# Forgetting attention and a gated convolution layer on one core: even partitions of q and k written by DMA, later weight loads, and the last output accumulated gate by gate

## The chip, the cores and the metric

The kernel runs on one core of a Trainium2 chip. The core has TensorE (PE), VectorE (DVE), ScalarE (ACT), GpSimd (POOL) and SyncE (SP), which here only issues DMAs, and 16 DMA engines. The metric is the device time in microseconds of one execution; a kernel's time is the median of its runs. A profile is of one execution and shows what each engine did when.

## The reference

Eight batches of eight heads, sequence length 576, head size 64. Attention with a forgetting gate comes first, and its heads side by side are the input of a feed-forward layer whose hidden units are gated by a convolution over the sequence.

```
scores = q @ k.T / 8
cum    = cumsum(log(clip(f, 1e-4, 1)))
scores = where(causal, -1e9, scores + cum[row] - cum[col])
x      = softmax(scores) @ v                  # heads side by side: (8, 576, 512)
h      = relu(x @ w_in)                       # 1024 hidden units
conv   = w[0]*h[s-1] + w[1]*h[s] + w[2]*h[s+1]
out    = (h * sigmoid(conv)) @ w_out          # (8, 576, 512), float32
```

## The kernel before

**Units of work.** A half batch `hb` is four heads of one batch; there are 16. Each has a q tile `stq` and a k tile `stk` of 128 partitions by 2304 columns (four heads of 576 positions) in bfloat16, in a ring of four buffers. All names and lines in this section are those of the kernel before.

**q and k in bfloat16 without a cast.** `load_qk` (L196) lets a DMA transpose read the float32 inputs as 16-bit halves. A head's 64 float32 values become 128 partitions: an odd partition holds the upper half of a value, which is the value in bfloat16, and an even one the lower half, which is no number. So the even partitions have to be overwritten before a matmul contracts over the 128 partitions. `clamp` (L202) does that in place, half a tile at a time (128 x 1152, so four calls for a half batch): it multiplies each partition by 1 or 0 and adds a constant, which leaves the odd partitions, clears the even ones and writes ones into two rows of `stq` (2 and 4) and minus one into row 0 of `stk`.

**The decay is in the same matmul.** With `kc`, the cumulated logarithm scaled for q's and k's side in two bfloat16 parts, copied to DRAM as `kd`, `rows_of` (L208, L210) writes one row of it to partition 0 of `stq` and two to partitions 2 and 4 of `stk`. The matmul over 128 partitions (L305) then gives the score with decay. Half batch 0 doesn't wait for that and adds the decay with two more matmuls each (L308, L310). The maximum isn't subtracted.

**Attention of a half batch.** Scores go to PSUM as a tail block, diagonal blocks and blocks off the diagonal. ScalarE takes the exponential (L317, L342, L332). GpSimd applies the causal mask to tail and diagonal blocks (L320, L345). For a whole batch, PE adds up the columns with a matrix of ones (`sums`), VectorE transposes and inverts the sums (L376, L377) and spreads them (L380); PE multiplies by v (`pv`), and VectorE normalises into `xt` (L389). v is loaded by `load_v` (L218) in five DMAs for a half batch, one for each block of 128 positions, and cast to float16 (L224, L226) on VectorE or GpSimd.

**Feed-forward of a batch.** For each of eight blocks `ff` of hidden units: PE multiplies by `w_in` (L399), ScalarE takes relu (L403), VectorE makes the convolution in two operations (L409, L411), ScalarE a tanh (L414), and VectorE forms the gated value `hg` (L418). When all eight are there, PE multiplies by `w_out` (L425, L430), ScalarE copies PSUM out (L438), and SP stores (L446, L449).

**The order of the work.** Nothing is scheduled at run time. `Plan` plays through all tasks of the kernel with assumed durations, keys as due times, and counts of free buffers, and so fixes each engine's order and, where a task may go to one of two engines, the engine. The instructions are then emitted in that order, and each engine works through its own in order. A DMA's issue holds its place in the queue of the engine that issues it: SP issues transposes, v and the output; POOL issues `kd`'s rows and the weights, which it converts to float16 on the way (L465); ACT issues a few at the start. A task waits for its inputs and for its buffers through semaphores. In `ps_t` there are four PSUM tiles of 1024 columns.

**Clamps' engine.** In half batches 1 and 2 a clamp may go to VectorE or GpSimd, and in all later ones it goes to GpSimd.

Of the kernel before, what the change touches and what calls it, by code (L numbers as in the profile page):

```python
# [11 lines left out]
BF16 = mybir.dt.bfloat16  # L12
# [102 lines left out]
def kernel(  # L115
# [21 lines left out]
    NFF = D_FF // 128  # L137
    SCALE = float(1.0 / (D ** 0.5))
    NHB = BH // 4
    HH = 4  # L140
    HS = HH * S
    RING, NP, NPT, NVA, NVF, NHT, NU, NOB = 4, 6, 4, 4, 3, 4, 3, 3
    AB = 256
# [7 lines left out]
    kd = dpool.tile([2, BH, S], BF16, name="kd")  # L151
# [8 lines left out]
    kc = cpool.tile([128, S], BF16, name="kc")  # L160
# [43 lines left out]

    def rows_of(hb):
        tq, tk = stq_t[hb % RING], stk_t[hb % RING]
        c = slice(hb * HH, (hb + 1) * HH)
        nc.gpsimd.dma_start(tq[0:1, 0:HS], kd[0:1, c, :].rearrange("j h s -> j (h s)"))  # L208
        row = HS + 64
        nc.gpsimd.dma_start(bass.AP(tensor=tk.tensor, offset=int(tk.offset) + 2 * row, ap=[[2 * row, 2], [1, HS]]),  # L210
                            kd[:, c, :].rearrange("j h s -> j (h s)"))

    def load_v(hb, t_load, eng):
        vf = vf_t[slot[t_load, "vf"]]
        base = int(v.offset) + hb * HH * S * D
        for kb in range(NKB):
            n = 128 if kb < NKB - 1 else SL
            eng.dma_start(vf[0:n, :, kb, :],  # L218
                          bass.AP(tensor=v.tensor, offset=base + kb * 128 * D, ap=[[D, n], [S * D, HH], [1, D]]))
# [17 lines left out]

    nc.gpsimd.iota(lii[:, 0:1], pattern=[[0, 1]], base=0, channel_multiplier=1)
# [23 lines left out]
    for t in range(RING):  # L262
        nc.gpsimd.memset(stk_t[t][:, HS:HS + 64], 0.0)
# [4 lines left out]
    nc.scalar.dma_start(kd[0], kc[0:BH])  # L268
    nc.scalar.dma_start(kd[1], kc[BH:128])
# [191 lines left out]
    def weights(pieces, dst, src, after, key, width):  # L461
        made = []
        for w in range(pieces):
            made.append(add({"POOL": 0.9}, after, key + 0.1 * w,
                            lambda me, w=w: nc.gpsimd.dma_start(  # L465
                                dst[:, :, width * w:width * (w + 1)],
                                src[:, :, width * w:width * (w + 1)]),
                            lag=2.0, dma=6.0 / pieces))
        return made
# [4 lines left out]
    for hb in range(NHB):  # L474
# [17 lines left out]
        if hb == 0:  # L492
            t_rows[hb] = None
        else:
            cl = []
            for p in range(2):
                for s in range(2):
                    cl.append(add({"POOL": 1.35, "DVE": 0.6} if hb < 3 else {"POOL": 1.35}, [t_ld[hb, s]], base - 1.0 + 0.1 * (2 * p + s),
                                  (lambda e, me, hb=hb, p=p, s=s: clamp(hb, p, s, e)) if hb < 3 else (lambda me, hb=hb, p=p, s=s: clamp(hb, p, s, nc.gpsimd))))
            t_rows[hb] = add({"POOL": 1.1}, cl, base - 0.8, lambda me, hb=hb: rows_of(hb), lag=2.5)  # L500
# [57 lines left out]
    for b in range(B):  # L558
        k1 = 4 * b + 5.0
        us = {}  # L560
        for ff in range(NFF):
# [12 lines left out]
            else:  # L574
# [3 lines left out]
                               give=[("ht", x)])  # L578
        done = [gates[b, ff] for ff in range(NFF)]
        for c in range(5):  # L580
            key = k1 + 4.2 + 0.8 * c
            if c in (0, 2, 4):
                t_o = x = add({"PE": 1.75 if c < 4 else 0.95}, done + t_wout, key,
                              lambda me, g0=g0, c=c: ffn2(me, g0, c), take=["ps"],
                              give=[("hg", g0)] if c == 4 else [])
            else:
                x = add({"PE": 1.75}, done, key, lambda me, t_o=t_o, g0=g0, c=c: ffn2(t_o, g0, c), behind=[t_o])
            if c in (1, 3, 4):
# [44 lines left out]
```

## Time and profile before

| | us |
|---|---|
| median of three runs | 336.97 |
| the runs | 333.33, 336.97, 337.31 |
| the profiled execution's own time | 335.01 |
| its span, first to last instruction | 333.3 |
| mean granted PE clock (1 is full) | 0.923 |

A page of the profile gives for each engine the time in which it was busy, its share of the span and the number of instructions. A group is all instructions of one line, engine and operation, with their tiles ("output<-inputs"), count, total and mean time. In a timeline a line gives the start, the time and the engine of one or more instructions that follow each other. A stage's line gives, for a stretch of the span, the busy time of PE, its weight loads (PEld), DVE, ACT and POOL with the number of instructions, and then the PE clock, the DMA engines' mean share and the rate in GB/s. The share of the DMA engines is the sum of their packets' times and can exceed 1 where packets overlap. A DMA queue's line gives its packets, its megabytes, and its packets' time as a share of 16 engines' span; q1 is SP's queue, q10 ACT's and q0 POOL's. A completion notice counts as a packet. Matmuls are pipelined, so a busy PE isn't one at its peak.

In this span the first L376 begins at 35.5 us and the others at 66.0, 104.9, 153.1, 191.6, 230.5, 262.6 and 291.7, one for each batch. The last gate (L418) ends at 320.8.

### The profile page before, as it was taken

Reading aid. Unit: us, or ns where it says so; the run is one execution under the profiler, and the core shown is the slowest. Engines: PE = TensorE matmul, PEld = TensorE weight load, DVE = VectorE, ACT = ScalarE, POOL = GpSimd, SP = SyncE. Lnnn points to the kernel's source line nnn. Section 1 sums busy time; section 2 is a strip of 40 time slices with the busy share of each in tenths; the row PEclk is TensorE's granted clock in tenths of the full one; section 3 lists DMA queues with packets and bytes.
Section 4 is the critical chain, followed back from the end, with each engine's and each line's share of the span. In section 5 each row is a group of like instructions: output and inputs, shape, how many; then the busy total and the mean of one; then the engine's idle time right before and its main releaser. Section 6 shows DMA issues by size and latency. Waiting matters only on the chain.

```text
span 333.3 us, 6984 instructions
## 1 busy us (share of the span) xinstructions
PE 259.6 (78%) x2832; PEld 177.3 (53%) x2832; DVE 279.2 (84%) x319; ACT 201.0 (60%) x267; POOL 184.8 (55%) x193
## 2 busy tenths in 40 slices
PE   0777956394955699699929998299979999979964
PEld 0555744273743564368704777147755775755622
DVE  4473899199999999897997799988999899799940
ACT  3166666373757674377906877178757888906822
POOL 4097799989999889304984069822881221100000
PEclk9997999698678989799996999879999999997979
DMA  8999999989996793319961589017301201100303
GB/s 174 232 195 194 196 198 195 197 133 221 220 177 104 94 218 96 120 65 223 149 140 63 83 177 181 2 65 151 73 4 63 76 9 63 66 18 0 128 16 142
DMA packets 126182, 40.97 MB, mean 123 GB/s; under 512 B 118693, under 2 KB 121893, under 8 KB 126150
## 3 DMA queue, kind: packets, MB, share of 16 engines
q1 hardware_dynamic: 118592, 37.76, 53.3%
q0 software_dynamic: 7232, 2.31, 6.2%
q10 hardware_dynamic: 326, 0.45, 0.5%
q8 instruction: 22, 0.36, 0.5%
q14 instruction: 10, 0.08, 0.1%
HBM read 14.15 MB, written 9.58 MB: 71 GB/s over the span
## 4 chain that ended last, share of the span: by engine, by line
DVE 38%; PE 35%; SPq 11%; issue 5%; DMA 4%; ACT 4%; POOL 2%; DVEq 0%; POOLq 0%; ACTq 0%
PE ps L425 13%; DVE hg L418 10%; DVE u L409 9%; PE ps L399 9%; SPq L196 8%; DVE u L411 8%; PE ps L366 7%; PE ps L305 5%; DVE va L224 3%; DMA vf<-in_v_dram 3%; DVE xt L389 3%; SPq L218 3%; DVE rb L380 2%; DVE va L226 1%; DMA stk<-kd 1%
## 5 line engine op out<-in xcount | busy, mean ns | idle before, releaser
L305 PE MATMUL ps<-stq,stk 128*128 128x128 bf16 (+3 forms) x576 | 64.7, 254 | 31.5 <-DVE stq L202 10.6
L399 PE MATMUL ps<-xt,w_in_f 128*128 128x288 f16 x512 | 77.5, 303 | 13.3 <-ACT ht L403 8.5
L414 ACT ACTIVATE hg<-u,cw 128x576 f16<-128x576 f32 x64 | 49.5, 776 | 62.2 <-DVE u L411 62.0
L425 PE MATMUL ps<-w_out_f,hg 128*128 128x512 f16 x256 | 66.7, 415 | 21.0 <-DVE hg L418 17.3
L418 DVE SCALAR_TENSOR_TENSOR hg<-hg,ht 128x576 f16<-128x576 f16 x64 | 67.1, 1057 | 9.1 <-ACT hg L414 8.9
L332 ACT ACTIVATE pp<-ps 128x1024 f16<-128x1024 f32 x64 | 64.1, 1022 | 12.2 <-PE ps L305 10.1
L409 DVE SCALAR_TENSOR_TENSOR u<-ht,cwt 128x576 f32<-128x576 f16 x64 | 67.5, 1066 | 4.4 <-ACT ht L403 4.4
L399 PEld LDWEIGHTS <-w_in_f 128*128 128x128 f16 x512 | 51.6, 103 | 33.6 <-issue 14.7
L411 DVE SCALAR_TENSOR_TENSOR u<-ht,cwt,u 128x576 f32<-128x576 f16 x64 | 65.7, 1037 | 0.8
L305 PEld LDWEIGHTS <-stk 128*128 128x128 bf16 x576 | 41.5, 104 | 44.3 <-issue 12.6
L345 POOL TENSOR_SCALAR_AFFINE_SELECT pp<-pd 128x1024 f16<-128x1024 f32 x32 | 39.6, 1236 | 33.8 <-ACT pd L342 33.1
L425 PEld LDWEIGHTS <-hg 128*128 128x128 f16 x256 | 26.3, 105 | 55.2 <-DVE hg L418 20.0
L202 POOL TENSOR_SCALAR stk<-stk,lim 128x1152 uint16<-128x1152 uint16 x29 | 50.5, 1744 | 0.5 <-DMA stk<-in_k_dram 0.5
L202 POOL TENSOR_SCALAR stq<-stq,lim 128x1152 uint16<-128x1152 uint16 x28 | 46.1, 1646 | 4.9 <-DMA stq<-in_q_dram 2.8
L403 ACT ACTIVATE ht<-ps 128x576 f16<-128x576 f32 x64 | 41.0, 651 | 12.4 <-PE ps L399 12.1
L320 POOL TENSOR_SCALAR_AFFINE_SELECT pt<-p 128x256 f16<-128x256 f32 x16 | 11.0, 689 | 60.1 <-ACT p L317 60.1
L342 ACT ACTIVATE pd<-ps 128x1024 f32<-128x1024 f32 x32 | 32.7, 1023 | 3.8 <-PE ps L305 2.1
L366 PE MATMUL ps<-pp,ones_h 128*64 128x128 f16 (+3 forms) x576 | 28.6, 249 | 1.0 <-POOL pp L345 0.6
L438 ACT COPY ob<-ps 128x1024 f32<-128x1024 f32 (+1 forms) x24 | 19.1, 796 | 14.7 <-PE ps L425 13.5
L366 PEld LDWEIGHTS <-ones_h 128*64 128x64 f16 x640 | 24.0, 116 | 7.0 <-issue 4.3
L366 PE MATMUL ps<-pp,va 128*64 128x128 f16 (+3 forms) x576 | 25.5, 241 | 2.6 <-DVE xt L389 2.6
L366 PEld LDWEIGHTS <-va 128*64 128x64 f16 x640 | 22.6, 111 | 6.7 <-issue 4.8
(66 smaller groups left out, 200.1 us busy)
## 6 DMA issues: line engine op xcount, KB each, us to landing
vf<-in_v_dram SPq DMA_DIRECT2D x64, 128.0 KB, 3.0
out_dram<-ob SPq DMA_DIRECT2D x16, 512.0 KB, 3.0
vf<-in_v_dram SPq DMA_DIRECT2D x16, 64.0 KB, 3.4
w_in_f<-in_moe_w_in_dram POOLq DMA_DIRECT2D x4, 256.0 KB, 5.6
w_out_f<-in_moe_w_out_dram POOLq DMA_DIRECT2D x4, 256.0 KB, 5.3
out_dram<-ob SPq DMA_DIRECT2D x16, 64.0 KB, 2.2
fsb<-in_f_dram ACTq DMA_DIRECT2D x2, 144.0 KB, 4.1
stq<-in_q_dram SPq DMA_TRANSPOSE x17, 5.9
```

Of the source, the lines that this page charges most:

```text
L202: eng.tensor_scalar(t, t, lim[:, 2 * side:2 * side + 1], lim[:, 2 * side + 1:2 * side + 2], op0=ALU.mult, op1=ALU.add)
L305: nc.tensor.matmul(o, tk[:, h * S + k0:h * S + k0 + 128], tq[:, h * S + q0:h * S + q0 + n], start=True, stop=hb > 0)
L332: nc.scalar.activation(pp_t[slot[t_dg, "p"]][:, 1024 * s:1024 * (s + 1)], ps_t[slot[t_sc, "ps"]], AF.Exp, scale=SCALE)
L345: nc.gpsimd.affine_select(pp_t[slot[t_dg, "p"]][:, 2048:3072].rearrange("p (m j) -> p m j", j=128), pd_t[slot[t_ex, "pd"]].rearrange("p (m ...
L366: nc.tensor.matmul(ps[64 * s:64 * (s + 1), AB + q0:AB + q0 + n], left_of(s, h, m), p, start=first and x in (0, 3), stop=last and x in (2, ...
L399: nc.tensor.matmul(ps[:, MB + 288 * a:MB + 288 * (a + 1)], w_in_f16[:, cc, 128 * ff:128 * (ff + 1)], xt[:, cc, 288 * a:288 * (a + 1)], sta ...
L403: nc.scalar.activation(ht_t[slot[t_m1, "ht"]][:, 1:1 + S], ps_t[slot[t_m1, "ps"]][:, MB:MB + S], AF.Relu, scale=0.5)
L409: nc.vector.scalar_tensor_tensor(u, ht[:, 0:S], cwt[:, ff, 0:1], ht[:, 1:1 + S], op0=ALU.mult, op1=ALU.add)
L411: nc.vector.scalar_tensor_tensor(u, ht[:, 2:2 + S], cwt[:, ff, 1:2], u, op0=ALU.mult, op1=ALU.add)
L414: nc.scalar.activation(hg_t[slot[t_g0, "hg"]][:, ff, :], u_t[slot[t_u, "u"]], AF.Tanh, scale=cw[:, ff, 1:2])
L418: nc.vector.scalar_tensor_tensor(hv, hv, 1.0, ht_t[slot[t_m1, "ht"]][:, 1:1 + S], op0=ALU.add, op1=ALU.mult)
L425: nc.tensor.matmul(o, hg[:, ff, 128 * c:128 * (c + 1)], w_out_f16[:, ff, :], start=(ff == 0), stop=(ff == NFF - 1))
```

## The change

**Even partitions by DMA.** From half batch 4 on there is no clamp. A new function `fill` overwrites the even partitions of `stq` or `stk` with two DMAs from SP: 61 rows (partitions 6, 8, ... 126) from a DRAM tile of zeros, `blank`, and three rows (partitions 0, 2 and 4) from DRAM tiles `kq` and `kk`, which hold `kd`'s rows and the rows of ones and minus ones. These DRAM tiles are written at the start from memsets in the fourth ring buffer, through POOL's queue, and from `kc`. Half batches 1 to 3 are still clamped, now all on VectorE, and `rows_of` is issued by SP.

**v's loads.** Still five DMAs for a half batch, but four of them are one head each (its first 512 positions); the fifth is as before.

**Due times.** The keys of q's and k's loads, of v's loads and of the last projection change. The weights' DMAs wait for other masks, and `w_in`'s are added one half batch later.

**The last batch's output.** `ffn2_last` accumulates `out` of batch 7 in three PSUM tiles, block by block, as each gate comes, behind the output of batch 6. Its PSUM tiles may be copied out by ScalarE or VectorE.

```diff
-    kd = dpool.tile([2, BH, S], BF16, name="kd")
+    kq = dpool.tile([3, BH, S], BF16, name="kq")
+    kk = dpool.tile([3, BH, S], BF16, name="kk")
+    blank = dpool.tile([61, HS], BF16, name="blank")
...
+    def even_rows(t, width, first, n):
+        return bass.AP(tensor=t.tensor, offset=int(t.offset) + first * width, ap=[[2 * width, n], [1, HS]])
+
+    def fill(hb, side):
+        t, width = ((stq_t, HS), (stk_t, HS + 64))[side]
+        t = t[hb % RING]
+        c = slice(hb * HH, (hb + 1) * HH)
+        nc.sync.dma_start(even_rows(t, width, 6, 61), blank)
+        nc.sync.dma_start(even_rows(t, width, 0, 3), (kq, kk)[side][:, c, :].rearrange("j h s -> j (h s)"))
+
     def rows_of(hb):
-        tq, tk = stq_t[hb % RING], stk_t[hb % RING]
         c = slice(hb * HH, (hb + 1) * HH)
-        nc.gpsimd.dma_start(tq[0:1, 0:HS], kd[0:1, c, :].rearrange("j h s -> j (h s)"))
...
+        nc.sync.dma_start(even_rows(stq_t[hb % RING], HS, 0, 1), kq[0:1, c, :].rearrange("j h s -> j (h s)"))
+        nc.sync.dma_start(even_rows(stk_t[hb % RING], HS + 64, 2, 2), kk[1:3, c, :].rearrange("j h s -> j (h s)"))
...
-        for kb in range(NKB):
-            n = 128 if kb < NKB - 1 else SL
-            eng.dma_start(vf[0:n, :, kb, :],
-                          bass.AP(tensor=v.tensor, offset=base + kb * 128 * D, ap=[[D, n], [S * D, HH], [1, D]]))
+        for h in range(HH):
+            eng.dma_start(vf[:, h, 0:4, :],
+                          bass.AP(tensor=v.tensor, offset=base + h * S * D, ap=[[D, 128], [128 * D, 4], [1, D]]))
+        eng.dma_start(vf[0:SL, :, 4, :],
+                      bass.AP(tensor=v.tensor, offset=base + 512 * D, ap=[[D, SL], [S * D, HH], [1, D]]))
...
+    nc.gpsimd.memset(stk_t[3], 0.0)
+    nc.gpsimd.memset(stq_t[3][0:BH, 0:S], 1.0)
+    nc.gpsimd.memset(stq_t[3][0:BH, S:2 * S], -1.0)
+    nc.gpsimd.dma_start(blank, stk_t[3][0:61, 0:HS])
+    for j in (1, 2):
+        nc.gpsimd.dma_start(kq[j], stq_t[3][0:BH, 0:S])
+    nc.gpsimd.dma_start(kk[0], stq_t[3][0:BH, S:2 * S])
...
-    nc.scalar.dma_start(kd[0], kc[0:BH])
-    nc.scalar.dma_start(kd[1], kc[BH:128])
+    nc.scalar.dma_start(kq[0], kc[0:BH])
+    nc.scalar.dma_start(kk[1], kc[0:BH])
+    nc.scalar.dma_start(kk[2], kc[BH:128])
...
+    def ffn2_last(t_o, g0, ff, a):
+        ps, hg = ps_t[slot[t_o, "ps"]], hg_t[slot[g0, "hg"]]
+        for j in range(2):
+            if a < 2:
+                c = 2 * a + j
+                nc.tensor.matmul(ps[:, 512 * j:512 * (j + 1)], hg[:, ff, 128 * c:128 * (c + 1)], w_out_f16[:, ff, :],
+                                 start=(ff == 0), stop=(ff == NFF - 1))
+            else:
+                nc.tensor.matmul(ps[64 * j:64 * (j + 1), 0:256], hg[:, ff, 512:576],
+                                 w_out_f16[:, ff, 256 * j:256 * (j + 1)],
+                                 start=(ff == 0), stop=(ff == NFF - 1), skip_group_check=True)
...
-                t_ld[hb, s] = add({"SP": 2.4}, old, base - 5.0 + 0.1 * s,
+                t_ld[hb, s] = add({"SP": 2.4}, old, base - 2.2 + 0.1 * s,
...
-        t_vl[hb] = add({"SP": 2.5}, [], base - 3.5, lambda me, hb=hb: load_v(hb, me, nc.sync), take=["vf"], lag=2.0,
+        t_vl[hb] = add({"SP": 2.5}, [], 4 * b + 2.4 + 0.1 * (hb % 2), lambda me, hb=hb: load_v(hb, me, nc.sync), take=["vf"], lag=2.0,
...
-            for p in range(2):
+            for p in range(2 if hb < NCL else 0):
...
+            fl = [add({"SP": 1.1}, cl, base - 0.8, lambda me, hb=hb: rows_of(hb), lag=2.3)] if cl else [add({"SP": 1.1}, [t_ld[hb, s]], base - 1.5 + 0.1 * s, lambda me, hb=hb, s=s: fill(hb, s), lag=2.3, dma=0.9)
+                  for s in range(2)]
...
-        if hb == 0:
-            t_win = weights(4, w_in_f16, moe_w_in.rearrange("(cc p) ff -> p cc ff", p=128), [t_mask[1]], 1.0, 256)
+        if hb == 1:
+            t_win = weights(4, w_in_f16, moe_w_in.rearrange("(cc p) ff -> p cc ff", p=128),
+                            [t_mask[1], t_mask[1], t_mask[2], t_mask[2]], 2.2, 256)
         if hb == 2:
-            t_wout = weights(4, w_out_f16, moe_w_out.rearrange("(ffc p) dm -> p ffc dm", p=128), [t_mask[3]], 4.0, 128)
+            t_wout = weights(4, w_out_f16, moe_w_out.rearrange("(ffc p) dm -> p ffc dm", p=128),
+                             [t_mask[3], t_mask[3], t_mask[4], t_mask[4]], 4.2, 128)
```

More of the change, by code (lines that the diff above doesn't have):

```diff
@@ L142 @@
     RING, NP, NPT, NVA, NVF, NHT, NU, NOB = 4, 6, 4, 4, 3, 4, 3, 3
+    NCL = 4
     AB = 256
@@ L203, in clamp @@
                           op0=ALU.mult, op1=ALU.add)
+    def even_rows(t, width, first, n):
[6 more added lines that the diff above has]
+        nc.sync.dma_start(even_rows(t, width, 0, 3), (kq, kk)[side][:, c, :].rearrange("j h s -> j (h s)"))
     def rows_of(hb):
-        tq, tk = stq_t[hb % RING], stk_t[hb % RING]
         c = slice(hb * HH, (hb + 1) * HH)
-        nc.gpsimd.dma_start(tq[0:1, 0:HS], kd[0:1, c, :].rearrange("j h s -> j (h s)"))
-        row = HS + 64
-        nc.gpsimd.dma_start(bass.AP(tensor=tk.tensor, offset=int(tk.offset) + 2 * row, ap=[[2 * row, 2], [1, HS]]),
-                            kd[:, c, :].rearrange("j h s -> j (h s)"))
+        nc.sync.dma_start(even_rows(stq_t[hb % RING], HS, 0, 1), kq[0:1, c, :].rearrange("j h s -> j (h s)"))
+        nc.sync.dma_start(even_rows(stk_t[hb % RING], HS + 64, 2, 2), kk[1:3, c, :].rearrange("j h s -> j (h s)"))
     def load_v(hb, t_load, eng):
@@ L261 @@
                                    op0=ALU.mult, op1=ALU.subtract)
-    for t in range(RING):
+    for t in range(RING - 1):
         nc.gpsimd.memset(stk_t[t][:, HS:HS + 64], 0.0)
@@ L463, in weights @@
         for w in range(pieces):
-            made.append(add({"POOL": 0.9}, after, key + 0.1 * w,
+            made.append(add({"POOL": 0.9}, [after[w]], key + 0.1 * w,
                             lambda me, w=w: nc.gpsimd.dma_start(
@@ L495 @@
             cl = []
-            for p in range(2):
+            for p in range(2 if hb < NCL else 0):
                 for s in range(2):
-                    cl.append(add({"POOL": 1.35, "DVE": 0.6} if hb < 3 else {"POOL": 1.35}, [t_ld[hb, s]], base - 1.0 + 0.1 * (2 * p + s),
-                                  (lambda e, me, hb=hb, p=p, s=s: clamp(hb, p, s, e)) if hb < 3 else (lambda me, hb=hb, p=p, s=s: clamp(hb, p, s, nc.gpsimd))))
-            t_rows[hb] = add({"POOL": 1.1}, cl, base - 0.8, lambda me, hb=hb: rows_of(hb), lag=2.5)
+                    cl.append(add({"DVE": 0.6}, [t_ld[hb, s]], base - 1.0 + 0.1 * (2 * p + s),
+                                  lambda me, hb=hb, p=p, s=s: clamp(hb, p, s, nc.vector)))
+            fl = [add({"SP": 1.1}, cl, base - 0.8, lambda me, hb=hb: rows_of(hb), lag=2.3)] if cl else [add({"SP": 1.1}, [t_ld[hb, s]], base - 1.5 + 0.1 * s, lambda me, hb=hb, s=s: fill(hb, s), lag=2.3, dma=0.9)
+                  for s in range(2)]
+            t_rows[hb] = add({"SP": 0.01}, fl, base - 1.2, lambda me: None, lag=0.0)
         slow = 3.0 if hb == 0 else 1.0
@@ L578 @@
                                give=[("ht", x)])
+        if b == B - 1:
+            t_o, evs = {}, {}
+            for ff in range(NFF):
+                for a in range(3):
+                    prev = t_o.get((ff - 1, a))
+                    t_o[ff, a] = add({"PE": 0.45 if a < 2 else 0.13}, [gates[b, ff], t_wout[-1], t_f2], k1 + 0.5 * ff + 3.0 + 0.1 * a,
+                                     lambda me, t_0=t_o.get((0, a)), g0=g0, ff=ff, a=a: ffn2_last(
+                                         me if t_0 is None else t_0, g0, ff, a),
+                                     take=["ps"] if ff == 0 else [], behind=[prev])
+            for a in range(3):
+                ev = add({"ACT": 1.05, "DVE": 1.2} if a < 2 else {"ACT": 0.4, "DVE": 0.4}, [t_o[NFF - 1, a]], k1 + 6.0,
+                         lambda e, me, t_0=t_o[0, a], a=a: evac(t_0, me, 2 * a, e), take=["ob"],
+                         give=[("ps", t_o[0, a])])
+                add({"SP": 0.6}, [ev], k1 + 6.0, lambda me, ev=ev, b=b, a=a: store(ev, b, 2 * a),
+                    give=[("ob", ev)], dma=1.6 if a < 2 else 0.4, lag=2.0)
+            continue
         done = [gates[b, ff] for ff in range(NFF)]
         for c in range(5):
-            key = k1 + 4.2 + 0.8 * c
+            key = k1 + 4.0 + (0.8 if b < B - 2 else 0.1) * c
             if c in (0, 2, 4):
@@ L587 @@
                 x = add({"PE": 1.75}, done, key, lambda me, t_o=t_o, g0=g0, c=c: ffn2(t_o, g0, c), behind=[t_o])
+            t_f2 = x
             if c in (1, 3, 4):
```

## The prediction

> **What bounds the kernel now.** I read the page's engine table and wait list, then the stages, then the timelines of two engines over one stall.
>
> ```profile
> PE 259.6 (78%) x2832; PEld 177.3 (53%) x2832; DVE 279.2 (84%) x319; ACT 201.0 (60%) x267; POOL 184.8 (55%) x193
> ```
>
> VectorE is the busiest, but its three gating operations do not take their own time: page and trace give a mean near 1.06 us for L409, L411 and L418, while undisturbed ones take 0.73, 0.74 and 0.67 us. The VectorE timeline, then the GpSimd timeline of the same microseconds (start, us, engine, line):
>
> ```profile
> 165.68 8.54 DVE L409 SCALAR_TENSOR_TENSOR u<-ht,cwt 128x576 f32<-128x576 f16 x2
> ```
>
> ```profile
> 168.67 1.10 POOL L345 TENSOR_SCALAR_AFFINE_SELECT pp<-pd 128x1024 f16<-128x1024 f32 x1
> 169.75 2.58 POOL L202 TENSOR_SCALAR stq<-stq,lim 128x1152 uint16<-128x1152 uint16 x2
> 172.33 1.29 POOL L202 TENSOR_SCALAR stk<-stk,lim 128x1152 uint16<-128x1152 uint16 x1
> ```
>
> Two operations worth 1.5 us take 8.5, and end as GpSimd's run of clamps ends at 173.6. The same follows at 207.66 (8.21 us for one L418). Next, stages from one transpose L376 to the next, i.e. one batch each (us, busy of PE, weight loads, DVE, ACT, POOL, PE clock, DMA share, GB/s):
>
> ```profile
> 153.00:191.60 38.60, 30.87 (x351) 20.75 (x348) 33.66 (x36) 23.88 (x33) 23.22 (x22) 0.91 0.63 120
> 191.60:230.50 38.90, 31.48 (x346) 20.74 (x345) 36.24 (x36) 24.44 (x34) 24.00 (x22) 0.91 0.49 110
> 262.60:291.70 29.10, 28.45 (x349) 20.23 (x348) 26.32 (x35) 24.21 (x34) 5.84 (x6) 1.00 0.12 43
> ```
>
> A batch costs 38.6 to 38.9 us with the clamps, and 29.1 once they are over. So clamps really are what the loop pays for, and 29 us is PE's own pace. The DMA queues and the issues, read because the change hands the clamps' work to them:
>
> ```profile
> q1 hardware_dynamic: 118592, 37.76, 53.3%
> q0 software_dynamic: 7232, 2.31, 6.2%
> q10 hardware_dynamic: 326, 0.45, 0.5%
> ```
>
> ```profile
> 141.00:145.00 4.00, 1.00 0.34 131
> 254.00:260.00 6.00, 1.00 0.28 105
> ```
>
> The engines are about 60% occupied on average. The last two lines (us, PE clock, DMA share, GB/s) are stretches in which only output is stored: 131/0.34/16 = 24.1 and 105/0.28/16 = 23.4 GB/s for one of the 16 engines. While q, k and v are loaded the share is about 1.0 at 195 GB/s, so an engine then moves only 12 GB/s.
>
> [...] ACT's two loads of f and two stores of kd have 64 rows each and cwrow has 3, which is 4*64+3 = 259 rows, and 326-259 = 67 completions = 4*16+3. For a number of rows that 16 engines don't divide, but exceeds 16, the trace of before has no case. [...] the stores above show 23 to 24. [...] The clock was 0.51 at 64 to 68 us, behind a 7 us wait[...].
>
> **The change part by part.**
>
> **Clamps leave GpSimd.** 57 of L202 on POOL, 96.6 us, go; VectorE does 16 instead of 7 (nine more at about 0.58 us, 5 us, in the first 50 us). Alone this is worth some 9 us in each of the disturbed batches.
>
> **The fill, hb 4 to 15.** Each side gets a blank of 61 rows of 4608 bytes (281 KB) and 3 data rows: 24 blanks and 24 small copies, all from SP. The built program carries the blank as 61 rows on both sides. [...] all 281 KB pass through one engine[...]. Price: [...] at most 281/23.5 = 12.0 us (stores in 2 KB and 1 KB pieces); the 12 GB/s of 256-byte pieces doesn't bind rows this long. I take 10.5. Below nothing it cannot be, for bytes are added to a queue. If all 16 shared it, 0.7 us. A small copy of 3 rows lands in about 2.6 us, as stk<-kd does, and adds little load.
>
> **What engine one has to move before the last blank has landed.** [...] Transposes: 32 equivalents of 590 KB, 2.03 us at the shortest issue, 2.9 usually; 2.5 taken: 80. v: 16 loads of the same bytes, 2.5: 40. Weights: 4.2 MB read at 195 GB/s: 21, less the overlap of queues: 18. Output of batches 0 to 5: 6*1.18 MB at 385 GB/s: 18. Blanks: 24*10.5 = 252. Sum 408. A blank waits for its transpose to land and the next transpose stands behind it in SP, so the engine runs dry now and then; about 1 us for each of 12 half batches: 12. Last blank at 420 us. All other work of those batches (PE 29 us a batch) is hidden behind it, where a half batch needs 5+2.5+1.5+21+1 = 31 us of that engine (transposes, v, stores, blanks, running dry), twice PE's pace for it.
>
> **From there to the end.** Scores and seven exponentials of the last half batch: 0.39+6*1.02, with the waits between them 8.5. Sums 0.8; L376 and L377 1.4; four spreads and norms at 0.71+0.69: 5.6; first projection and relu 2.5; the gating chain 8*(0.73+0.74+0.67) = 17.1; last output 5.2 (next part); a slow PE clock 1. Together 42. 420+42 = 462, plus 1.7 between the span (333.3) and its own run (335.01) = 464. The median of the three runs is 336.97, 0.6% above that run. I say 465.
>
> **Last batch's output accumulated as gates come.** Before: last gate ends at 320.8, then 7.07+1.01 us of PE, a copy of 1.0, a store of about 3. After: six matmuls of the last gate, 1.2, copies on two engines 1.0, the store 3: 5.2 against 12.5. It gains 7 us, at the very end, and PE has 10 idle us in the last stage to do it in. Three of four PSUM tiles are held by it, so the last projection has one; that can take back 1 or 2.
>
> **Weights later; v by head; keys.** Before, the w_in pieces were issued at 24.7, 34.0, 74.2 and 96.0 us behind clamps; in the order built, two stand behind the second diagonal mask, one behind the fourth and one behind the sixth, with no clamps between, so the last ones arrive sooner despite the name. v moves the same bytes in the same 256-byte pieces: nothing. Both are hidden behind the blanks; with those spread, the weights make the first two batches' projection possible 30 us sooner.
>
> **Start.** POOL now first clears stk3 and issues four DMAs ahead of the iota; VectorE's first operations wait for iota and the scan for f stands behind them. By L271 (0.30 us for 256 columns) 2368 columns cost 2.5, the rest 2 to 3; f was read at 5.6 us. About 2.5 us later, uncovered.
>
> **SP's queue.** It gains 54 issues of 0.5 to 0.6 us, 30 us, and each blank's wait for its transposes; stores and v stand behind those. Before, SP had 128 us of waiting for output copies, so the issues alone fit.
>
> **The rivals.** (1) **The blanks are spread over 16 engines**[...]. Then a blank is 0.7 us and GpSimd's disturbance is gone: first L376 at 35.5+2.5, seven batches at 30.5 (29.1, and 1.4 for casts now mostly on GpSimd, two of 1.04 and 0.39 us a batch, half of which meet a gating operation), tail 41.6-7 = 34.6: 38+213.5+34.6+1.7 = 288. It decides below about 3 us a blank, where the engine's half batch (9+6+1 = 16) comes down to half of 30.5. For it speaks the 29.1 us stage; against it the count of q10. (2) **Blanks are spread, but SP's order binds**: per batch four transposes 11.6, ten v issues 5.8, eight fill issues 4.8, stores 2.4 = 24.6, and if no landing is covered four waits of 3 us (5.9 to land, 2.9 of it in the issue): 36.6. 38+7*36.6+34.6+1.7 = 330, about the old time. Against it: four buffers of q and k let loads run a batch and more ahead.
>
> **How the numbers follow.** One engine for the blanks: 0.82, 405 to 545 ([...] at 12.0 with transposes at 2.9, v at 2.9 and 3 us dry per half batch: 288+93+46+39+36+42 = 544). Spread: 0.14, 275 to 305. SP's order: 0.04, 315 to 340. The range 405 to 545 is the first case's, with its bounds; the other two are left out with 0.18 and a fiftieth at the edges. Faster by over 2%: 0.15; within: 0.02; slower: 0.83. Two per cent, 7 us, is about what three runs with a spread of 1.2% can tell.
>
> **What would show it.** Right: the DMA share low, near a tenth to a third, over long stretches of the span while PE waits for stq or stk from blank; a median landing of the blank copies of 10 us and more (more with the queue); in q1 the blanks post 24 completions, not 384; L409, L411 and L418 at 0.7 to 0.8 us; batches some 60 us apart from the third on; the last gate to the end in 6 us. Wrong: blanks landing in 3 to 4 us and batches 30 us apart. A blank at half or twice the price moves the time by 125 to 250 us.

## The result and the profile after

The changed kernel takes 509.13 us (507.46 to 509.96, 4 runs) against 335.15 us (333.26 to 337.31, 4 runs) for the kernel before: 1.518 times as long, 95% interval 1.505 to 1.531. Its profiled execution took 509.74 us, of which 508.0 are the span. The ratios in this document leave out executions more than 1.5% above the fastest of their kernel, and four of the profiles used further down are of such executions: the split in 48 + 13 rows (315.5 us), that in 57 + 4 (355.8), and the kernels with all clamps on VectorE (307.7 for the changed kernel, 306.8 for the kernel before). All lines of this section are of the changed kernel's profiled execution, and the line numbers are those of the changed code (L199 the transposes, L215 the blank, L216 the three rows behind it, L227 and L229 v, L324 the scores, L395 the transpose of the sums).

First the page's engine table and DMA queues.

```profile
PE 270.4 (53%) x2832; PEld 184.4 (36%) x2832; DVE 232.6 (46%) x320; ACT 200.0 (39%) x266; POOL 99.9 (20%) x121
...
q1 hardware_dynamic: 120242, 44.88, 65.0%
q0 software_dynamic: 6448, 2.60, 4.1%
q10 hardware_dynamic: 406, 0.53, 0.4%
```

No engine is above 53%. GpSimd has lost 85 us and VectorE 47, and the kernel is 174 us longer, so the time went into waiting. The 7.1 MB more in q1 are the blanks and the rows behind them: 24*(281,088+13,824) bytes, and a little for half batches 1 to 3. The packets of q1 tell how they were divided. It has 1650 more than before: by their sizes in the two traces, 1545 more of 4608 bytes, which are the rows, and 105 more of 4 bytes, the completions of the prediction (the 67 that it counts in q10 are 67 packets of 4 bytes as well). With one completion to a blank, the additions are 24*(61+1) for the blanks, 24*(3+3) for the rows behind them, and 3*(1+1) + 3*(2+2) for the rows of half batches 1 to 3: 1488 + 144 + 18 = 1650, with 24 + 72 + 9 = 105 completions. With sixteen completions to a blank it would be 2010.

The chain of waits (by engine, then by line) and the PE's entries in the list of who waited (us in total, times, longest):

```profile
SPq 38%; DMA 28%; PE 22%; DVE 5%; ACT 4%; issue 3%; POOL 0%; ACTq 0%; POOLq 0%; DVEq 0%
SPq L199 18%; DMA stk<-kk 12%; SPq L227 9%; PE ps L418 7%; DMA stk<-blank 7%; SPq L216 6%; PE ps L385 4%; PE ps L324 4%; DMA vf<-in_v_dram 3%; PE ps L444 3%; DMA out_dram<-ob 3%; DMA stk<-in_k_dram 2%; SPq L229 2%; SPq L215 2%; PE ps L458 1%
```

```profile
PE ps L324 <- DMA stk<-kk: 83.1, 5, 24.6
...
PEld L324 <- DMA stk<-blank: 60.9, 4, 24.8
...
PE ps L324 <- DMA stk<-blank: 46.2, 4, 17.8
```

Two thirds of the chain is DMA and SP's queue, and PE's scores wait up to 25 us at a time for a blank or for the small copy of rows behind it. One such stretch in the window view (us, PE busy, PE clock, DMA share, GB/s), and SP's timeline a little later (start, us, instruction):

```profile
105.00:111.00 6.00, 0.66 (x6) 0.90 0.06 25
114.00:118.00 4.00, 0.00 (x0) 0.50 0.06 26
121.00:124.00 3.00, 0.00 (x0) 0.50 0.06 26
```

```profile
130.38 0.64 SPq L215 DMA_DIRECT2D stq<-blank  x1
...
131.85 0.57 SPq L215 DMA_DIRECT2D stk<-blank  x1
...
133.30 21.65 SPq L199 DMA_TRANSPOSE stq<-in_q_dram  x1
```

A share of 0.06 is one engine of sixteen (1/16 = 0.0625). Both blanks of that half batch had been issued by 103.4 us, so two copies with different destinations are in flight and still only one engine moves bytes, at 25 to 26 GB/s. At that rate a blank takes 281/26 = 10.8 us. PE stands still and its clock is at 0.50. The blanks themselves cost SP 0.6 us each; the transpose behind two of them holds SP for 21.65 us, and v and the output stores stand behind that.

The stages from one L395 to the next (us, busy of PE, PEld, DVE, ACT, POOL, PE clock, DMA share, GB/s):

```profile
260.50:301.90 41.40, 31.31 (x322) 21.50 (x322) 26.65 (x36) 22.18 (x30) 9.57 (x11) 0.84 0.68 96
301.90:361.80 59.90, 31.68 (x344) 21.56 (x341) 28.99 (x36) 24.81 (x34) 11.15 (x11) 0.78 0.80 102
361.80:429.80 68.00, 34.61 (x353) 23.10 (x353) 26.29 (x34) 24.50 (x33) 8.66 (x11) 0.72 0.67 81
429.80:469.70 39.90, 30.42 (x349) 21.09 (x348) 27.04 (x35) 24.19 (x34) 5.57 (x6) 0.87 0.19 68
469.70:508.00 38.30, 29.95 (x248) 16.78 (x247) 29.50 (x41) 16.57 (x25) 0.00 (x0) 0.97 0.19 66
```

A batch has 30 to 35 us of PE work in these stages and takes 38 to 68 us (103.5, with 37 us of PE work, in the one before these). From the first L395, at 42.7 us, to the seventh, at 429.8, the mean is 64.5 us. Last, the gating operations on VectorE, of which the page before had means near 1.06 us:

```profile
L428 DVE SCALAR_TENSOR_TENSOR u<-ht,cwt 128x576 f32<-128x576 f16 x64 | 57.9, 915 | 18.4 <-ACT ht L422 17.7 <-ACT hg L433 0.8
L430 DVE SCALAR_TENSOR_TENSOR u<-ht,cwt,u 128x576 f32<-128x576 f16 x64 | 56.3, 888 | 0.9
L437 DVE SCALAR_TENSOR_TENSOR hg<-hg,ht 128x576 f16<-128x576 f16 x64 | 52.5, 826 | 110.6 <-ACT hg L433 110.3
```

Their means did fall, by 0.15 to 0.23 us, and L437 now waits 110 us for ScalarE, which is itself busy for 39% of the span. What went are the few long ones: the longest L437 takes 2.0 us where the longest L418 of the kernel before took 8.2, while the median is 0.75 us in both.

### The profile page after: what moved, and what is told of

Same layout as the page of the kernel before. It is cut to its first block, busy times and chain, and to the rows that moved or that the text cites. A ratio compares the mean times of both kernels' runs of the same rounds, so it can differ in the third digit from the quotient of the medians.

```text
span 508.0 us, 6941 instructions
## 1 busy us (share of the span) xinstructions
PE 270.4 (53%) x2832; PEld 184.4 (36%) x2832; DVE 232.6 (46%) x320; ACT 200.0 (39%) x266; POOL 99.9 (20%) x121
## 4 chain that ended last, share of the span: by engine, by line
SPq 38%; DMA 28%; PE 22%; DVE 5%; ACT 4%; issue 3%; POOL 0%; ACTq 0%; POOLq 0%; DVEq 0%
SPq L199 18%; DMA stk<-kk 12%; SPq L227 9%; PE ps L418 7%; DMA stk<-blank 7%; SPq L216 6%; PE ps L385 4%; PE ps L324 4%; DMA vf<-in_v_dram 3%; PE ps L444 3%; DMA out_dram<-ob 3%; DMA stk<-in_k_dram 2%; SPq L229 2%; SPq L215 2%; PE ps L458 1%
## 5 line engine op out<-in xcount | busy, mean ns | idle before, releaser
L324 PE MATMUL ps<-stq,stk 128*128 128x128 bf16 (+3 forms) x576 | 70.6, 265 | 159.3 <-DMA stk<-kk 83.1
L418 PE MATMUL ps<-xt,w_in_f 128*128 128x288 f16 x512 | 84.6, 319 | 44.8 <-DVE st L395 25.5
L324 PEld LDWEIGHTS <-stk 128*128 128x128 bf16 x576 | 43.9, 109 | 174.6 <-issue 90.5
L437 DVE SCALAR_TENSOR_TENSOR hg<-hg,ht 128x576 f16<-128x576 f16 x64 | 52.5, 826 | 110.6 <-ACT hg L433 110.3
L418 PEld LDWEIGHTS <-w_in_f 128*128 128x128 f16 x512 | 53.6, 108 | 68.9 <-issue 47.8
L351 ACT ACTIVATE pp<-ps 128x1024 f16<-128x1024 f32 x64 | 64.5, 1026 | 17.6 <-PE ps L324 13.6
L428 DVE SCALAR_TENSOR_TENSOR u<-ht,cwt 128x576 f32<-128x576 f16 x64 | 57.9, 915 | 18.4 <-ACT ht L422 17.7
L336 ACT ACTIVATE p<-ps 128x256 f32<-128x256 f32 x16 | 6.2, 388 | 134.0 <-PE ps L324 120.1
L430 DVE SCALAR_TENSOR_TENSOR u<-ht,cwt,u 128x576 f32<-128x576 f16 x64 | 56.3, 888 | 0.9
L444 PE MATMUL ps<-w_out_f,hg 128*128 128x512 f16 x224 | 53.6, 388 | 1.7 <-DVE hg L437 1.6
L235 POOL CAST va<-vf 128x1024 f16<-128x1024 f32 x14 | 16.1, 1148 | 190.2 <-DMA vf<-in_v_dram 177.4
L339 POOL TENSOR_SCALAR_AFFINE_SELECT pt<-p 128x256 f16<-128x256 f32 x16 | 21.8, 1360 | 99.1 <-ACT p L336 99.1
L444 PEld LDWEIGHTS <-hg 128*128 128x128 f16 x224 | 22.2, 100 | 26.5 <-DVE hg L437 2.3
```

Source lines behind the costliest of these rows:

```text
L324: nc.tensor.matmul(o, tk[:, h * S + k0:h * S + k0 + 128], tq[:, h * S + q0:h * S + q0 + n], start=True, stop=hb > 0)
L351: nc.scalar.activation(pp_t[slot[t_dg, "p"]][:, 1024 * s:1024 * (s + 1)], ps_t[slot[t_sc, "ps"]], AF.Exp, scale=SCALE)
L418: nc.tensor.matmul(ps[:, MB + 288 * a:MB + 288 * (a + 1)], w_in_f16[:, cc, 128 * ff:128 * (ff + 1)], xt[:, cc, 288 * a:288 * (a + 1)], sta ...
L428: nc.vector.scalar_tensor_tensor(u, ht[:, 0:S], cwt[:, ff, 0:1], ht[:, 1:1 + S], op0=ALU.mult, op1=ALU.add)
L430: nc.vector.scalar_tensor_tensor(u, ht[:, 2:2 + S], cwt[:, ff, 1:2], u, op0=ALU.mult, op1=ALU.add)
L437: nc.vector.scalar_tensor_tensor(hv, hv, 1.0, ht_t[slot[t_m1, "ht"]][:, 1:1 + S], op0=ALU.add, op1=ALU.mult)
```

## The experiments

**How many engines carry the blank.** The share of 0.06 shows one engine at work. That it is one because no number from 2 to 16 divides 61 is a guess (the divisor rule of the texts below), which these runs test: the engines of a copy would be the largest number up to 16 that divides its rows. The same bytes were therefore sent to the same rows in two copies, cut at three places. By the guess the busiest engine then has 30, 20 or 4 rows. The edit, with n = 58, 57 and 48:

```
-        nc.sync.dma_start(even_rows(t, width, 6, 61), blank)
+        nc.sync.dma_start(even_rows(t, width, 6, n), blank[0:n])
+        nc.sync.dma_start(even_rows(t, width, 6 + 2 * n, 61 - n), blank[n:61])
```

> The blank as 58 rows and 3 rows. One-engine theory with the divisor rule: 58 = 2*29, two engines; the busiest moves 30 rows, 5.4 us, a half batch needs about 21 us of it, 11 less than the changed kernel: 509-12*11 = 375 us (350 to 400). q1 has 24*(2+3-1) = 96 packets more. Rival, SP's waits: 505 to 525 us.

> The blank as 57 rows and 4 rows. One-engine theory with the divisor rule: 57 = 3*19, so 57 rows go to 3 engines and 4 rows to 4; the busiest moves 20 rows, 3.6 us, a half batch needs about 9+7.2+1 = 17 us of it, 15 less than with 61 rows on one, so 509-12*15 = 329 us (305 to 350). If an engine count is not tied to a divisor (16 engines whenever there are 16 rows), this equals the 48 and 13 split. Rival, SP's waits: 505 to 525 us.

> The blank of 61 rows is issued as two DMAs, of 48 and of 13 rows; same bytes, same order, 24 issues more on SP (0.6 us each). One-engine theory: 48 rows go to 16 engines and 13 rows to 13, so the busiest engine moves 4 rows (0.7 us at the 11 us that 61 rows took), and the time falls to about 290 us (280 to 310), q1 has 24*(16+13-1) = 672 packets more than the changed kernel. Rival, the waits in SP's order (each blank waits for its transposes to land, and stores and v stand behind): nothing of that is changed but for 14 us of issues, so the time stays at 505 to 525 us.

| pieces | rows on the busiest engine, as expected | packets of q1 over those of the changed kernel | time, us | ratio to before | longest SP issue of a transpose, 60 to 300 us |
|---|---|---|---|---|---|
| 61 | 61 | 0 | 509.13 | 1.518 [1.505, 1.531] | 21.65 us |
| 58 + 3 | 29 + 1 | 96 = 24*(2+3-1) | 387.89 | 1.154 [1.148, 1.160] | 12.63 us |
| 57 + 4 | 19 + 1 | 144 = 24*(3+4-1) | 351.12 | 1.040 [1.034, 1.047] | 8.78 us |
| 48 + 13 | 3 + 1 | 672 = 24*(16+13-1) | 309.68 | 0.920 [0.914, 0.925] | 4.47 us |

The packets of q1 rise by the number expected each time (to 120,338, 120,386 and 120,914), and the time falls though SP issues 24 copies more. From 61 rows to 20 it falls by 158.0 us, which is 158.0/24 = 6.6 us a blank for 41*4608 bytes = 189 KB: 28.7 GB/s, close to the 25 to 26 seen in flight. The three times lie 13 to 22 us above the middle of what was expected, and 57 + 4 lies 1 us outside its range; where that is lost is taken up below and only in part settled.

**Is it the engine, or SP's queue?** In all of these the blank stands in the queue in which the transposes follow. The blank and the three rows behind it were moved to the other hardware queue, ScalarE's, and in another kernel to GpSimd's. The edit for ScalarE (for GpSimd `nc.gpsimd` and `"POOL"`):

```
-        nc.sync.dma_start(even_rows(t, width, 6, 61), blank)
-        nc.sync.dma_start(even_rows(t, width, 0, 3), (kq, kk)[side]...)
+        nc.scalar.dma_start(even_rows(t, width, 6, 61), blank)
+        nc.scalar.dma_start(even_rows(t, width, 0, 3), (kq, kk)[side]...)
...
-            fl = [...] if cl else [add({"SP": 1.1}, [t_ld[hb, s]], base - 1.5 + 0.1 * s, ...)
+            fl = [...] if cl else [add({"ACT": 1.1}, [t_ld[hb, s]], base - 1.5 + 0.1 * s, ...)
```

> The changed kernel with the blank and the 3 rows behind it issued from ScalarE's queue: a hardware queue as SP's is, so that the 61 rows should stay undivided, but no blank stands in SP's queue. Theory (the one engine that carries all rows sets the time, and the transposes, which need that engine too, wait for it from whatever queue the blank came): that queue's packets rise by some 68 for each of 24, a blank lands 10 us or more after its issue, transposes still hold SP for over 10 us at times, and the time is 440 us or more (ScalarE, whose exponentials stand behind the blank's wait for its transpose, may add to it). Rival (blank and transpose hinder each other only within one queue): 310 to 400 us. If the time comes to 300 to 325 us with a landing below 6 us, ScalarE's queue divides what SP's does not.

> The changed kernel with the blank and the 3 rows behind it issued from the GpSimd queue and not from SP's; their bytes, rows and destinations as they were. Theory (the one engine that carries all 61 rows sets the time): if this queue too gives 61 rows one engine, a blank still takes 10 to 12 us of it and the time stays at 440 to 515 us, with the transposes no longer held on SP's queue. Rival (what costs is SP's queue, held 12 to 22 us at a transpose behind a blank): 310 to 400 us. If this queue splits the 61 rows over the engines, its blanks land in 2 to 4 us, its packets rise by far more than 61 a blank and the time is 295 to 325 us; then it is the split and not the queue, too.

From ScalarE: 511.16 us (508.83 to 515.71), ratio 1.527 [1.516, 1.537], practically the changed kernel's own time. Its queues, and SP's timeline:

```profile
q1 hardware_dynamic: 118610, 37.80, 79.4%
q10 hardware_dynamic: 2038, 7.61, 4.2%
```

```profile
166.57 17.36 SPq L199 DMA_TRANSPOSE stq<-in_q_dram  x1
...
227.73 19.07 SPq L199 DMA_TRANSPOSE stk<-in_k_dram  x1
```

q10 has 1632 packets more than in the changed kernel, 24*(61+1+3+3). SP holds no blank any more, and its transposes still stand for 17 and 19 us. So it isn't the order in a queue: the transpose needs the engine that is busy with the blank. (The total alone would show less, for ScalarE's own work now stands behind a blank's wait for its transpose, up to 31 us at a time.)

From GpSimd: 303.15 us (302.93 to 304.0), ratio 0.907 [0.898, 0.915]. The queue, and the issues of the blanks (KB, median us to landing):

```profile
q0 software_dynamic: 9136, 9.68, 17.7%
```

```profile
stq<-blank POOLq DMA_DIRECT2D x12, 274.5 KB, 4.7
stk<-blank POOLq DMA_DIRECT2D x12, 274.5 KB, 5.2
```

The same 61 rows, bytes and destinations land in 4.7 to 5.2 us, where one engine at 28.7 GB/s would need 9.8, and from 100 to 200 us the longest issue of a transpose on SP is 4.7 us. q0 rises by 2688 packets, 24*112, where the hardware queues had 24*68: this queue divides the copy. Over how many engines isn't settled by these figures. It is the third of the expected cases. Batches run at (263.12-109.30)/5 = 30.8 us from the third L395 on.

**The other half of the change alone: clamps off GpSimd, without blanks.** Twice: in the changed kernel, cleaning all half batches on VectorE; and in the kernel before, with nothing else touched.

```
-    NCL = 4
+    NCL = 16
```

> All half batches are cleaned by clamps on VectorE, none by the blanks; the rest of the change stays. One-engine theory: the loss goes with the blanks, GpSimd's disturbance is gone as well, and VectorE has 48 clamps of 0.58 us more, 3.5 us a batch for six batches, on an engine with about 27 of 30 us used: 300 us (285 to 320). Rival, that the loss lies in the other parts (late weights, v's order, stores ahead of loads in SP's queue): stays above 400 us.

```
-    cl.append(add({"POOL": 1.35, "DVE": 0.6} if hb < 3 else {"POOL": 1.35}, [t_ld[hb, s]], ...
+    cl.append(add({"DVE": 0.6}, [t_ld[hb, s]], ..., lambda me, ...: clamp(hb, p, s, nc.vector)))
```

> The kernel before with one edit: every clamp from the second half batch on is planned on VectorE alone. Theory (GpSimd's clamps slow the gating on VectorE and hold its own queue, some 9 us in each disturbed batch): in the run with all clamps on VectorE the batches came 29.5 to 30.6 us apart against about 38 before; that run has a slower first 85 us (17 us at the second row of reciprocals) and a shorter tail (some 7 us), neither of which this kernel has. So 305.8 - 17 + 7 = 296 us (286 to 308), batches 29 to 31 us apart, gating operations near 0.85 us. Rival (the clamps are hidden beside PE and what made that run fast was the order of v and the weights): 328 to 340 us.

The changed kernel with clamps: 305.8 us, ratio 0.902 [0.897, 0.907]. The kernel before with clamps on VectorE: 302.82 us (300.13 to 306.83), ratio 0.901 [0.895, 0.908], a little above the 296 expected and inside the range. So the move of the clamps is worth 33 us by itself, with v, weights and tail as they were. Four batches, from the fourth L376 on, in the kernel before (where the window ends 1.7 us short of the eighth L376) and in this one (columns as above), then the gating operations before and in this one:

```profile
153.10:290.00 136.90, 117.83 (x1346) 80.28 (x1344) 126.40 (x138) 95.73 (x130) 71.06 (x63) 0.95 0.40 88
```

```profile
145.00:263.00 118.00, 114.03 (x1368) 80.16 (x1367) 115.52 (x159) 96.86 (x131) 41.20 (x48) 1.00 0.47 102
```

```profile
L409 DVE SCALAR_TENSOR_TENSOR u<-ht,cwt 128x576 f32<-128x576 f16 x64 | 67.5, 1066 | 4.4 <-ACT ht L403 4.4
L411 DVE SCALAR_TENSOR_TENSOR u<-ht,cwt,u 128x576 f32<-128x576 f16 x64 | 65.7, 1037 | 0.8
L418 DVE SCALAR_TENSOR_TENSOR hg<-hg,ht 128x576 f16<-128x576 f16 x64 | 67.1, 1057 | 9.1 <-ACT hg L414 8.9
```

```profile
L409 DVE SCALAR_TENSOR_TENSOR u<-ht,cwt 128x576 f32<-128x576 f16 x64 | 56.3, 891 | 0.0
L411 DVE SCALAR_TENSOR_TENSOR u<-ht,cwt,u 128x576 f32<-128x576 f16 x64 | 54.2, 857 | 0.2
L418 DVE SCALAR_TENSOR_TENSOR hg<-hg,ht 128x576 f16<-128x576 f16 x64 | 49.1, 776 | 8.2 <-ACT hg L414 8.2
```

VectorE takes on 57 more clamps of 0.68 us over the kernel. In these four batches, where some 20 more operations run on it, its busy time still falls by 11 us. With the fourth batch taken whole, the gating operations take 82 us instead of 101, and three casts of v (4.9 us) have gone to GpSimd, against 13.6 us of clamps. Again it is the long ones that went: the medians of L409, L411 and L418 are 0.81, 0.81 and 0.75 us here and 0.81, 0.82 and 0.75 before, the longest 1.8, 1.6 and 1.6 us here and 6.9, 2.4 and 8.2 before. How much of the 33 us comes of that, and how much of masks and casts that no longer stand behind clamps in GpSimd's own queue, wasn't separated. The batches come 29.5 us apart, with PE granted its full clock. The first L376, though, is at 44.5 us instead of 35.5.

**The last batch's output, alone and with the clamps.** The second kernel below has both edits. In the third the clamps of half batches 1 and 2 keep the choice of engines that they had, because of that late first L376. The tail is the change's `ffn2_last`, with its plan entries, put into the kernel before as it stands.

```
+        if b == B - 1:
...
+                    t_o[ff, a] = add({"PE": 0.45 if a < 2 else 0.13}, [gates[b, ff], t_wout[-1], t_f2], ...
```

> The kernel before with only the last batch's output accumulated as its gates come. Theory (the prediction's step: from the last gate to the end 12.5 us becomes 5.2, later measured as 8.0 in the changed kernel): 4 to 7 us less than before, 331 us (328 to 334). Rival (PE is no longer the last to finish, so nothing is gained): 335 to 338 us.

> The kernel before with the clamps on VectorE and the last batch's output accumulated as its gates come; keys, v and weights as before, no blanks. The two gains add: 296 - 6 = 290 us (280 to 303). If the gain of the first were that of the order of v and weights: 325 to 335 us.

```
-    {"POOL": 1.35, "DVE": 0.6} if hb < 3 else {"POOL": 1.35}
+    {"POOL": 1.35, "DVE": 0.6} if hb < 3 else {"DVE": 0.6}
```

> The kernel before with the last batch's output accumulated as its gates come, and the clamps of half batches 3 to 15 alone on VectorE; those of half batches 1 and 2 keep the choice of two engines that they had. Theory (with every clamp on VectorE the first batches were 4 to 9 us late, since VectorE waits in its queue for transposes that land late; the later batches came 29 us apart): reciprocals at 36, 67, 103 as in the kernel before, then 29 us apart to 248, and 38 us more: span 287, time 289 us (284 to 297). Rival (the early delay is paid anyway, by the transposes): 297 to 304 us.

The tail alone: 334.3 us (331.27 to 336.65, 14 runs), ratio 0.998 [0.994, 1.001]: no difference that these runs show, where 4 to 7 us were expected; the time lies between the ranges of the theory and the rival. The end of the kernel before, then the end of this one (start, us, instruction, in brackets what it waited for):

```profile
320.04 0.76 DVE L418 SCALAR_TENSOR_TENSOR hg<-hg,ht 128x576 f16<-128x576 f16 x1 [0.17 <-ACT hg L414]
...
325.59 3.83 SPq L446 DMA_DIRECT2D out_dram<-ob  x2
...
327.86 1.06 PE L430 MATMUL ps<-w_out_f,hg 128*64 128x256 f16 x16
```

```profile
318.85 0.76 DVE L418 SCALAR_TENSOR_TENSOR hg<-hg,ht 128x576 f16<-128x576 f16 x1 [0.18 <-ACT hg L414]
...
324.09 0.30 PE L442 MATMUL ps<-w_out_f,hg 128*64 128x256 f16 x2
...
324.85 0.98 SPq L458 DMA_DIRECT2D out_dram<-ob  x2
325.92 2.04 SPq L461 DMA_DIRECT2D out_dram<-ob  x2
```

PE finishes 4.8 us after the last gate instead of 8.1: it has not kept up with the gates, and four gates' accumulations of 1.2 us each come after the last gate. And from PE's end to the end of the span it is 330.5-324.4 = 6.1 us instead of 333.3-328.9 = 4.4, since all of the output now goes to SP after 324.85, when PE is done, where before its first part was sent from 325.59 on, while PE still had 3 us to go. Of the 3.3 us gained, 1.7 go back.

Both together: 301.68 us (298.02 to 305.26), ratio 0.897 [0.890, 0.904], not told apart from the clamps alone; 290 was expected. With the first clamps left where they were: 295.78 us (294.57 to 298.28), ratio 0.885 [0.876, 0.894], the lowest here, though its interval still touches that of both edits. Its first L376 is at 35.9 us, against 39.5 in the kernel with both edits and 44.5 with the clamps alone, so the early delay goes with VectorE's first clamps. By what wait they cause it isn't settled: the two kernels that have it differ by 5 us, though VectorE's order up to L376 is the same in both. It stays 7 us above what was expected, because its last five batches are 30.4 us apart ((255.27-103.35)/5) and not 29.

**Where the split version loses its first 100 us.** In the kernel with pieces of 48 and 13 rows the second transpose of the sums (L396 there) is at 84.9 us, against 66.0 in the kernel before. v, the keys of the transposes, and the weight loads were given back what they had before.

```
-        t_vl[hb] = add({"SP": 2.5}, [], 4 * b + 2.4 + 0.1 * (hb % 2), ...
+        t_vl[hb] = add({"SP": 2.5}, [], base - 3.5, ...
...
-                t_ld[hb, s] = add({"SP": 2.4}, old, base - 2.2 + 0.1 * s, ...
+                t_ld[hb, s] = add({"SP": 2.4}, old, base - 5.0 + 0.1 * s, ...
...
-        if hb == 1:
-            t_win = weights(4, ..., [t_mask[1], t_mask[1], t_mask[2], t_mask[2]], 2.2, 256)
+        if hb == 0:
+            t_win = weights(4, ..., [t_mask[1]] * 4, 1.0, 256)
```

> The changed kernel with the blank in two pieces of 48 and 13 rows, as run before at 309.7 us, and the transposes, v and the weight loads given back the keys, pieces and masks of the kernel before. Theory (its slow first 110 us come of weights and v that load late and together with the first transposes): the second row of reciprocals near 68 us instead of 85 and 293 us in all (285 to 300). Rival (the slow start is that of the constants made on GpSimd, the rows on SP and the clamps on VectorE): 305 to 315 us.

306.3 us (305.85 to 307.92), ratio 0.915 [0.910, 0.920], against 0.920 [0.914, 0.925]. The time lies in the rival's range and not in the theory's. The second transpose does come earlier, at 73.9 us, but the third is at 116.9 where it was at 112.3, and the intervals overlap. So the order of v and weights moves the delay about, and isn't shown to make it. The blanks don't make it either: in the changed kernel without them the second L395 is at 82.5 us. With nothing but the clamps moved in the kernel before, the second L376 is at 78.5, and with the last output's edit besides at 74.2, so a good part of the delay appears with the clamps on VectorE (one execution each). The rows on SP and the constants on GpSimd weren't separated.

## Why the prediction was right, and where its sum was off

The likeliest case was the one that happened, and the range held the time. By its steps:

**One engine carries all 61 rows: right, and shown.** By packets (one completion a blank), by the share of 0.06 with two blanks in flight, by the three cuts, and by the run from ScalarE's queue. Ahead of the result no trace showed it: it was the author's assumption. With one completion for each engine, the packets fit 1 engine for 61 rows, and, as sums of two pieces, 2 for 58 with 3 for 3, 3 for 57 with 4 for 4, and 16 for 48 with 13 for 13; the 67 completions of q10 in the kernel before fit 16 for 64 rows and 3 for 3. Each of these is the largest number up to 16 that divides the rows. That the blanks of a half batch pass through the same engine, which the sum needed, is borne out by the share of 0.06 with two of them in flight; which of the sixteen it is, no view here shows.

**10.5 us a blank: right.** It was an estimate below the 12.0 us that the stores gave, and the range's lower end, 405 us, was one too. In flight 281 KB at 26 GB/s are 10.8 us; the difference between the cuts gives 281/28.7 = 9.8.

**31 us of that engine for each half batch: right.** From the first blank's issue at 66.5 us to PE's start behind the last, at 446.8, it is 380 us for 12 half batches: 31.7. Two blanks at 9.8 to 10.8 us leave 10 to 12 us for the rest, for which the sum had 10; its single terms (transposes, v, stores, running dry) weren't measured apart, and it took all other transfers to load this engine as much as any of the sixteen, which isn't shown.

**Last blank at 420: 27 us too early.** The sum counted only the bytes of that engine and left 420-12*31 = 48 us for everything ahead of the first blank. The first blank is issued at 66.5 us, behind v and transposes that take 5 to 7 us each to issue while weights are loaded beside them, after a start that was itself late: that is 18.5 us. The other 8.3 are 12 times the 0.69 us by which a half batch is longer.

**From there to the end, 42 us: it was 61.** The sum let the last half batch's scores and exponentials run alone (9.3 us with the sums). In the trace PE has batch 6's projections between them, for both had waited for the same blank, and the last L395 comes 469.7-446.8 = 23 us after PE's restart. That mis-sizes this step by 13.6 us. From L395 to the end of the last gate it is 30.4 us, against 26.6 for the terms of the sum and 1 for a slow clock: 2.8. From the last gate to the end 7.9 instead of 5.2: 2.7. Together 19. These and the 27 above are the whole distance from the sum's 464 to 509.7. Both parts were too short, so the range was not met by errors that cancel.

**Clamps off GpSimd, some 9 us a disturbed batch: right.** Alone, they take the two batches from which this was read from 38.5 and 38.9 us to 29.3 and 28.5. The two behind them, of 32.1 and 29.1 us, were little disturbed and gain 1.1 and 0.3. In the changed kernel this is hidden behind the blanks, as was said. The sign of gating operations at 0.7 to 0.8 us mixed two measures: the 0.73, 0.74 and 0.67 us are steps from one start to the next. By the trace's own durations the median operation takes 0.75 to 0.82 us in all these kernels, and the means, 0.83 to 0.92 in the changed one, are raised by long ones of up to 2 us.

**Last output, 7 us: wrong.** It took for granted that PE has room to follow the gates: 1.2 us of PE after the last one, but it is 1.8 in the changed kernel and 4.8 where this edit stood alone. And it put the copies and the store at 4 us, but from PE's end to the end of the span it is 6.1 in both. Alone the edit shows no measurable gain.

**Start, 2.5 us: right for the wait, not for its sequel.** (Scaled from 0.30 us for 256 columns, the clearing of 2368 comes to 2.8 us and not 2.5; it took 2.1.) PE's first scores wait 13.3 us for VectorE instead of 10.6, but the first L395 is 7.2 us late. In the kernel before, clamps of the early half batches on VectorE alone put it 4 to 9 us late, and leaving those of half batches 1 and 2 as they were takes that away.

**Weights later; v by head:** expected to be hidden, and the weights a help once the blanks are spread. The `w_in` pieces are issued at 34 to 47 us instead of 25 to 96, so they do come sooner. With the blanks in two pieces, v, transposes and weights in their old order give 306.3 against 309.7 us, no clear difference; no gain from the new order is shown.

**The rival that the blanks are spread** fell for the changed kernel, but its price can be compared: 288 us expected, 303 to 310 measured where they are spread. Its 30.5 us a batch is right (30.8 from GpSimd's queue); the first two batches are what it missed, with the second L395 at 81.3 instead of 68.5 us. That SP's order would bind at 330 us fell too: with 24 issues more than the changed kernel, the 48 + 13 split takes 309.7.

**The sign "a DMA share of a tenth to a third over long stretches"** held only in part. It is 0.06 where blanks alone move, but 0.75 where a transpose waits for the busy engine (last section). The batches, expected some 60 us apart from the third on, came 68 us apart. Landing times of the blanks aren't given in that profile; the evidence for them is the waits.

## What to carry to other kernels

Before a copy is issued from SP or ScalarE, factor its number of rows: an edit that cleans 61 rows with one instruction looked cheap here at 0.6 us of queue and cost some 10 us of an engine that the transposes behind it needed too. Cut it into pieces whose row counts divide well (48 + 13 rows brought 509.13 us down to 309.68), or issue it from GpSimd (303.15 us), and read the packets of the queue to see what was done. When work leaves a contended engine, test that alone first: here the clamps on VectorE gave 33 us in the kernel before, and 31 us with the rest of the change around them, so that the rest, blanks apart, brought nothing more that these runs show.

## What was not expected of the hardware

- While a transpose waits for one busy engine, the DMA share reads 0.75 at 33 GB/s (134 to 154 us of the changed kernel), where a full stage has about 1.0 at over 200 GB/s (1.09 at 211, 141 to 172 us with the blanks on GpSimd's queue). The share alone would have called that stretch well used.
- A single-engine copy stops transposes of another queue about as long as those of its own (21.65 us): 17 to 19 us on SP with the blanks on ScalarE's queue.
- GpSimd's queue divides a copy of 61 rows that both hardware queues leave whole: 4.7 to 5.2 us to land, 303 us instead of 509 to 511.
